# Attention output matrix of branch B built in natural row order and put into q's order by transfers within SBUF

## The chip, the cores and the metric

The kernel runs on one core of one Trainium2 chip. The metric is device time in microseconds: the median of the runs, and for reading, one profiled execution with every instruction of every engine. TensorE (PE) multiplies matrices and writes to PSUM only; PEld is its weight load, which overlaps the matmuls. VectorE (DVE) and ScalarE (ACT) compute on SBUF and PSUM, GpSimd (POOL) works only at the start, and SyncE (SP) issues most of the DMA transfers. Every engine works through its own queue in order.

## The reference

Two linear-attention blocks, A and B, share the input x (2048 tokens, 640 features) and are mixed by a gate. Each has 32 heads of 20 features.

```python
def _A_ref(x, wqkv, wo):              # _B_ref is the same with B's weights
    qkv = (x @ wqkv).reshape(B, S, 3, H, Dh).transpose(2, 0, 3, 1, 4)
    q, k, v = qkv[0], qkv[1], qkv[2]
    phi = lambda t: jnp.where(t > 0, t + 1, jnp.exp(t)) + 1e-6
    pq, pk = phi(q), phi(k)
    kv = jnp.einsum("bhsd,bhse->bhde", pk, v)
    z = jnp.einsum("bhsd->bhd", pk)
    num = jnp.einsum("bhqd,bhde->bhqe", pq, kv)
    den = jnp.einsum("bhqd,bhd->bhq", pq, z)[..., None] + 1e-6
    return (num / den).transpose(0, 2, 1, 3).reshape(B, S, D) @ wo

x = A_x
g = sigmoid((x * gate_w).sum(-1, keepdims=True))
return g * _A_ref(x, A_wqkv, A_wo) + (1 - g) * _B_ref(x, B_wqkv, B_wo)
```

## The kernel before

The kernel never forms v. For each branch it computes G = x^T phi(k) (640 by 640, tiles `GT`), then per head kv = wv^T G, then M = blockdiag(kv) @ wo (640 by 640, tiles `M[0]` and `M[1]`). The gate and the reciprocal of the denominator are multiplied into phi(q), which lies transposed in `pqT[0]` and `pqT[1]` (features on partitions, five chunks). The result is then pqA @ M_A + pqB @ M_B, a product with inner size 1280.

**q's order.** Chunk c, partition p of `pqT` holds feature 5p + c (`mixed`, L246). M must have its rows in the same order: natural row r belongs on partition r // 5, chunk r % 5.

**M_A** (`kv_a` L430, `m_a` L448) is made among the key chunks of branch B. Heads are taken in blocks of six, six and four to each half of the features (`WB`, 120, 120 and 80 rows): 30 matmuls give the kv blocks in PSUM, four VectorE multiplications with the mask put them into `KVA`, and for each of the six blocks two matmuls of 320 columns give rows of M_A in natural order. ScalarE copies a block to a stage in `GT`, SP writes it to a scratch tensor in DRAM (L461), and a last transfer (L463) loads all of it in q's order.

**M_B** is made later, between the last Strassen product of G (`g_strassen`, L330) and the products of the last stage. Groups of four heads are used (`KG` = 80): `kvt_mm` (L413) makes four blocks per half, 20 matmuls, `kvt_mask` (L422) masks them into `KVT`, and `m_half` (L472) makes 128 rows of one chunk in q's order directly, with eight matmuls 32 columns wide per half (80 in all), whose weights take every fifth column. ScalarE (one half: VectorE) copies them to `M[1]`.

**The last stage** computes the product of inner size 1280 by Winograd's form of Strassen's scheme. Tokens are split into lower and upper 1024, the inner size into A and B, the columns into two halves of 320. A `Pair` (L573) holds tokens i*128 of the lower and of the upper half; there are eight pairs, with seven products of five matmuls each (`prod`, L559):

- P1 = pqA(lower) by M_A's left half; P2 = pqB(lower) by M_B's left half; P3 = s4 by M_B's right half; P4 = pqB(upper) by TM3; P5 = s1 by TM0; P6 = s2 by TM1; P7 = D3 by TM2.
- s1, s2, s4 are sums of parts of `pqT`, which `p_sums` (L509) makes for two pairs at a time as its k = 1, 2, 4 (VectorE, 128x1280); s2 and s4 lie in `xT`. TM0 to TM3 are sums of M's quarters (`m_sums`, L520; TM0 at L740).
- P1's result is copied by ScalarE to `p1s` and P6 accumulates onto it in the same bank x; ScalarE copies that to `u2`; VectorE adds P7 to make `u3`, and four more sums (`c22`, `c11`, those of P4 and P3) make the four output quarters. P4 accumulates onto P7 in bank y, P3 onto P5 in bank z; P2 is in bank w.

There are eight PSUM banks: z, x, w and y, one for even and one for odd pairs. In this kernel each of the eight is a tile of its own (`acc`, L733 and L765). Before the w and y banks are opened, the pools `mid` and `single` use their space for kv and M_B; `kv` there is one tile of two banks. The tail from L700 on is under a manual schedule: each engine's queue has the order in which the lines are written.

## Time and profile before

| | |
|---|---|
| median of 3 runs | 189.83 us (189.77 to 190.37) |
| span of the profiled execution, first to last instruction | 188.1 us |
| PE busy | 182.7 us, 97% of the span, 1460 matmuls |
| PE weight loads | 123.5 us, 66% |
| DVE busy | 150.3 us, 80%, 244 instructions |
| ACT busy | 75.0 us, 40% |
| granted TensorE clock | 1.000 over the span |
| DMA | 15.63 MB, mean 83 GB/s |

The span is counted inside the device time; 1.7 us of the median lie around it. Busy time of PE is counted from modelled ends, so 97% means that its queue is nearly always supplied. The chain of waits follows the work that ended last back to its start; in the timeline a line gives start, duration, engine, source line, operation, tiles written and read, shape, and in brackets the idle time before it and what ended that.

### The profile page before, as it was taken

What the parts mean: (1) busy time and instruction counts of PE and PEld (TensorE: products, weight loads), DVE (VectorE), ACT (ScalarE), POOL (GpSimd) and SP (SyncE); (2) the same over time, 40 slices, a digit from 0 to 9 for tenths busy, and PEclk for the clock granted to TensorE, in tenths of its full rate; (3) what the DMA queues carried; (4) which work ended last, traced back from release to release, by engine and by line L of the source; (5) the groups of instructions that cost most, each with busy time, mean ns of one, the idle gap of its engine ahead of it and who ended that gap; (6) DMA issues with size and microseconds to landing.
All of it is one profiled execution on the core that took longest, in us unless ns stands there. A gap on an engine that the chain in (4) does not pass through costs nothing.

```text
span 188.1 us, 3574 instructions
## 1 busy us (share of the span) xinstructions
PE 182.7 (97%) x1460; PEld 123.5 (66%) x1465; DVE 150.3 (80%) x244; ACT 75.0 (40%) x106; POOL 2.8 (2%) x17
## 2 busy tenths in 40 slices
PE   8899999999999999999999999999999999999992
PEld 3566657755577677877765555576778776777772
DVE  1378968899998999799889997739699989787553
ACT  2055446457942501367674577422401611111110
POOL 6000000000000000000000000000000000000000
PEclk9999999999999999999999999999999999999999
DMA  5975447992140000011115000000543003211222
GB/s 184 320 124 94 105 84 250 360 249 87 16 164 0 3 0 0 3 33 33 54 44 189 2 0 0 3 0 0 178 112 62 3 3 112 97 70 56 87 71 71
DMA packets 19802, 15.63 MB, mean 83 GB/s; under 512 B 9546, under 2 KB 19658, under 8 KB 19786
## 3 DMA queue, kind: packets, MB, share of 16 engines
q1 hardware_dynamic: 18922, 14.59, 29.0%
q10 hardware_dynamic: 864, 0.82, 1.3%
q8 instruction: 11, 0.18, 0.4%
q14 instruction: 5, 0.04, 0.1%
HBM read 10.00 MB, written 3.44 MB: 71 GB/s over the span
## 4 chain that ended last, share of the span: by engine, by line
PE 93%; DMA 3%; DVE 1%; ACTq 0%; issue 0%; ACT 0%; DVEq 0%
PE gs L325 16%; PE kB L207 12%; PE qB L256 11%; PE kA L207 11%; PE qA L256 7%; PE ox L563 6%; PE oy L563 5%; PE oz L563 5%; PE qA L267 5%; DMA xn<-in_A_x_dram 3%; PE ow L563 3%; PE gB L298 2%; PE gA L298 2%; DVE osb L568 1%; PE mA L456 1%; PE mid L417 1%
## 5 line engine op out<-in xcount | busy, mean ns | idle before, releaser
L207 PEld LDWEIGHTS <-xT 128*128 128x128 bf16 x320 | 31.0, 98 | 12.4 <-DVE xT L192 0.5
L200 DVE TENSOR_SCALAR e<-e 128x640 bf16<-128x640 bf16 (+1 forms) x52 | 18.7, 360 | 6.3 <-ACT e L197 5.7
L207 PE MATMUL kB<-wkB,xT 128*128 128x320 bf16 x160 | 23.0, 299 | 0.0
L207 PE MATMUL kA<-wkA,xT 128*128 128x320 bf16 x160 | 22.6, 299 | 0.1
L256 PE MATMUL qB<-xT,wqB 128*128 128x512 bf16 x98 | 21.7, 379 | 0.1
L197 ACT ACTIVATE e<-kB 128x640 bf16<-128x640 f32 x16 | 11.3, 704 | 18.8 <-PE kB L207 17.5
L256 PEld LDWEIGHTS <-wqB 128*128 128x128 bf16 x100 | 11.7, 117 | 9.8 <-issue 0.2
L197 ACT ACTIVATE e<-kA 128x640 bf16<-128x640 f32 x16 | 11.0, 704 | 13.3 <-PE kA L207 13.3
L204 DVE SCALAR_TENSOR_TENSOR pk<-kA,e 128x640 bf16<-128x640 f32 x16 | 13.2, 825 | 1.7
L204 DVE SCALAR_TENSOR_TENSOR pk<-kB,e 128x640 bf16<-128x640 f32 x16 | 13.2, 825 | 1.7
L197 ACT ACTIVATE e<-qA 128x1024 bf16<-128x1024 f32 x10 | 10.2, 1023 | 9.3 <-PE qA L267 3.7
L197 ACT ACTIVATE e<-qB 128x1024 bf16<-128x1024 f32 x10 | 10.2, 1023 | 8.7 <-PE qB L256 8.4
L256 PE MATMUL qA<-xT,wqA 128*128 128x512 bf16 x59 | 13.2, 379 | 0.1
L607 ACT COPY u<-ox 128x320 f32<-128x320 f32 x8 | 3.4, 425 | 21.9 <-PE ox L563 21.9
L325 PEld LDWEIGHTS <-S 128*128 128x128 bf16 x96 | 9.4, 98 | 3.6
L325 PEld LDWEIGHTS <-xn 128*128 128x128 bf16 x96 | 9.1, 98 | 4.0 <-issue 0.4
L256 PEld LDWEIGHTS <-wqA 128*128 128x128 bf16 x60 | 7.0, 117 | 5.8
L563 PEld LDWEIGHTS <-xT 128*128 128x128 bf16 x85 | 8.0, 98 | 3.1 <-DVE xT L502 0.2
L591 ACT COPY p1s<-ox 128x320 f32<-128x320 f32 x8 | 3.4, 426 | 16.6 <-PE ox L563 16.6
L563 PEld LDWEIGHTS <-pqTA 128*128 128x128 bf16 x85 | 7.9, 98 | 2.9 <-issue 0.2
L563 PEld LDWEIGHTS <-pqTB 128*128 128x128 bf16 x80 | 7.8, 98 | 3.0
L325 PE MATMUL gs<-pk,xn 128*128 128x320 bf16 x64 | 9.4, 300 | 0.0
(124 smaller groups left out, 285.2 us busy)
## 6 DMA issues: line engine op xcount, KB each, us to landing
out_dram<-osb SPq DMA_DIRECT2D x14, 160.0 KB, 1.8
xn<-in_A_x_dram SPq DMA_DIRECT2D x3, 640.0 KB, 6.8
wqA<-in_A_wqkv_dram SPq DMA_DIRECT2D x1, 800.0 KB, 7.3
wvA<-in_A_wqkv_dram SPq DMA_DIRECT2D x1, 800.0 KB, 11.8
wkB<-in_B_wqkv_dram SPq DMA_DIRECT2D x1, 800.0 KB, 6.3
wqB<-in_B_wqkv_dram SPq DMA_DIRECT2D x1, 800.0 KB, 4.8
MA<-ma_dram SPq DMA_DIRECT2D x1, 800.0 KB, 4.3
wvB<-in_B_wqkv_dram SPq DMA_DIRECT2D x1, 800.0 KB, 5.7
```

The lines of the kernel that those rows point to most:

```text
L197: nc.scalar.activation(out=e[:], in_=src, func=ACT.Exp)
L200: nc.vector.tensor_scalar(e[:], e[:], 1.0, EPS, op0=ALU.min, op1=ALU.add)
L204: nc.vector.scalar_tensor_tensor(out=dst, in0=src, scalar=1.0 + EPS, in1=e[:], op0=ALU.add, op1=ALU.max)
L207: nc.tensor.matmul(pt[:, hf, 0:HF], lhsT=xT[:, c, i * P:(i + 1) * P], rhs=wk[b][:, c, hf * HF:(hf + 1) * HF], start=(c == 0), stop=(c == D ...
L256: nc.tensor.matmul(pt[:, u, :], lhsT=mixed(wq[b][:, c, :], m), rhs=xT[:, c, n * HB:(n + 1) * HB], start=(c == 0), stop=(c == DT - 1),)
L267: nc.tensor.matmul(pt[:, u, :], lhsT=mixed(wq[b][:, c, :], m + u), rhs=xT[:, c, n * HB:(n + 1) * HB], start=(c == 0), stop=(c == DT - 1),)
L298: nc.tensor.matmul(pt[:, hf, 0:HF], lhsT=xn[:, i, c * P:(c + 1) * P], rhs=pk[:, i, hf * HF:(hf + 1) * HF], start=(i == 0), stop=(i == ST - 1),
L325: nc.tensor.matmul(pt[:, n, 0:HF], lhsT=left[:, i, n * P:(n + 1) * P], rhs=right[:, i, :], start=(first and i == 0), stop=(i == hc - 1), s ...
L417: nc.tensor.matmul(pt[:KG, hf, j * KG:(j + 1) * KG], lhsT=wv[b][:, c, (4 * hf + j) * KG:(4 * hf + j + 1) * KG], rhs=GT[hf][:, c, j * KG:(j ...
L563: nc.tensor.matmul(dst, lhsT=left[:, c, r0:r0 + P], rhs=right[:, c, :], start=(first and c == 0), stop=(c == DT - 1), skip_group_check=not ...
L591: nc.scalar.copy(out=self.p1s[:], in_=self.at("x"))
L607: nc.scalar.copy(out=self.u2[:], in_=self.at("x"))
```

## The change

- M_B is made as M_A is: `kv_mm` and `kv_mask` (blocks of 120, 120, 80 rows, into `KVA`), then `m_rows` for each of six blocks: two matmuls, a copy of the rows to a stage (in `pk`, free by then), and one transfer from SBUF to SBUF that puts 120 or 80 rows on 24 or 16 partitions of `M[1]`, in q's order. The copies are ACT's, DVE's, ACT's, DVE's, ACT's, and for the last block one half each.
- M_A uses the same function: its rows go from SBUF to `M[0]` directly, without the scratch tensor in DRAM and the load from it.
- The eight PSUM banks of the last stage are opened at once, as four tiles z, x, w, y of two banks each; `acc` holds their halves. kv of B and the six blocks use them first.
- P1 of pairs 2, 3 and 4 is moved ahead of the first P2, into free halves of w and y. Its result is kept in `pk`, and P6 of these pairs no longer accumulates onto it: VectorE adds P6 and `p1s` to make `u2`, in place of ScalarE's copy.
- TM0 is made earlier, in `g_all` ahead of `rec_pass`; the other TM sums are three instructions over the whole tile where there were fifteen by chunks.
- wo of B is loaded by four transfers in place of one; `KVT`, its memset and the scratch tensor go.

```diff
@@
-KG = 80
-NG = 8
...
-    KVT = persist.tile([P, 4, 3, KG], BF16, name="KVT")
...
-    ma_dram = scratch.tile([D, D], BF16, name="ma_dram")
...
-    nc.vector.memset(KVT[:], 0.0)
...
@@ -410,75 +404,54 @@
         )
         return zsel
 
-    def kvt_mm(b, pt, hf):
-
-        for j in range(4):
+    def kv_mm(b, hf, dst):
+
+        for i, w in enumerate(WB):
+            d0 = i * WB[0]
             for c in range(DT):
                 nc.tensor.matmul(
-                    pt[:KG, hf, j * KG:(j + 1) * KG], lhsT=wv[b][:, c, (4 * hf + j) * KG:(4 * hf + j + 1) * KG],
-                    rhs=GT[hf][:, c, j * KG:(j + 1) * KG], start=(c == 0), stop=(c == DT - 1),
+                    dst[:w, d0:d0 + w], lhsT=wv[b][:, c, hf * HF + d0:hf * HF + d0 + w],
+                    rhs=GT[hf][:, c, d0:d0 + w], start=(c == 0), stop=(c == DT - 1),
                 )
 
-    def kvt_mask(pt, hf):
-
-        nc.vector.tensor_tensor(
-            out=KVT[:KG, 2 * hf:2 * hf + 2, 0:3:2, :],
-            in0=pt[:KG, hf, 0:HF].rearrange("p (g k n) -> p g k n", g=2, k=2),
-            in1=maskE[:KG, None, None, 0:KG].to_broadcast([KG, 2, 2, KG]), op=ALU.mult,
-        )
+    def kv_mask(hf, src):
+
+        for i, n in ((0, 2), (2, 1)):
+            w = WB[i]
+            nc.vector.tensor_tensor(
+                out=KVA[:w, 3 * hf + i:3 * hf + i + n, 0:w],
+                in0=src[:w, i * WB[0]:i * WB[0] + n * w].rearrange("p (i n) -> p i n", i=n),
+                in1=maskE[:w, None, 0:w].to_broadcast([w, n, w]), op=ALU.mult,
+            )
 
     def kv_a():
 
         pt = ps("kvA")
         for hf in range(2):
-            for i, w in enumerate(WB):
-                d0 = i * WB[0]
-                for c in range(DT):
-                    nc.tensor.matmul(
-                        pt[:w, hf, d0:d0 + w], lhsT=wv[0][:, c, hf * HF + d0:hf * HF + d0 + w],
-                        rhs=GT[hf][:, c, d0:d0 + w], start=(c == 0), stop=(c == DT - 1),
-                    )
+            kv_mm(0, hf, pt[:, hf, :])
         for hf in range(2):
-            for i, n in ((0, 2), (2, 1)):
-                w = WB[i]
-                nc.vector.tensor_tensor(
-                    out=KVA[:w, 3 * hf + i:3 * hf + i + n, 0:w],
-                    in0=pt[:w, hf, i * WB[0]:i * WB[0] + n * w].rearrange("p (i n) -> p i n", i=n),
-                    in1=maskE[:w, None, 0:w].to_broadcast([w, n, w]), op=ALU.mult,
-                )
-
-    def m_a(k):
+            kv_mask(hf, pt[:, hf, :])
+
+    def m_rows(b, k, pt, stage, engines):
 
         hf, i = divmod(k, 3)
-        w, d0 = WB[i], hf * HF + i * WB[0]
-        pt = ps("mA")
+        w, p0 = WB[i], (hf * HF + i * WB[0]) // DT
         for n in range(2):
             nc.tensor.matmul(
-                pt[:w, n, 0:HF], lhsT=KVA[:w, k, 0:w], rhs=wo_sb[0][:w, k, n * HF:(n + 1) * HF], start=True, stop=True,
+                pt[:w, n, 0:HF], lhsT=KVA[:w, k, 0:w], rhs=wo_sb[b][:w, k, n * HF:(n + 1) * HF], start=True, stop=True,
             )
-        part = GT[k % 2][:, k // 2 % 2 * 2:k // 2 % 2 * 2 + 2, :]
-        nc.scalar.copy(out=part[:w], in_=pt[:w, :, 0:HF])
-        nc.sync.dma_start(out=ma_dram[d0:d0 + w, :], in_=part[:w].rearrange("p b n -> p (b n)"))
-        if k == NW - 1:
-            nc.sync.dma_start(out=M[0][:], in_=ma_dram[:].rearrange("(p c) f -> p c f", c=DT))
-
-    def m_unit(b, c, eng, pt=None):
-
-        pt = ps("mA") if pt is None else pt
-        for hf in range(2):
-            m_half(b, c, hf, pt[:, hf, 0:HF])
-        evac(M[b][:, c, :], pt, eng)
-
-    def m_half(b, c, hf, dst):
-
-        for k in range(2):
-            for g in range(4):
-                heads = KVT[:KG, g, k:k + 2, :].rearrange("p x n -> p (x n)")
-                nc.tensor.matmul(
-                    dst[32 * g:32 * g + 32, :], lhsT=mixed(heads, c),
-                    rhs=wo_sb[b][:KG, 2 * g + k, hf * HF:(hf + 1) * HF], start=(k == 0), stop=(k == 1),
-                    tile_position=(0, 32 * g),
-                )
+        if len(engines) == 1:
+            copy = nc.scalar.copy if engines[0] == "act" else nc.vector.tensor_copy
+            copy(out=stage[:w], in_=pt[:w, :, 0:HF])
+        else:
+            for n, eng in enumerate(engines):
+                copy = nc.scalar.copy if eng == "act" else nc.vector.tensor_copy
+                copy(out=stage[:w, n], in_=pt[:w, n, 0:HF])
+        nc.sync.dma_start(out=M[b][p0:p0 + w // DT, :, :], in_=stage[:w].rearrange("p b n -> p (b n)"))
+
+    def m_a(k):
+
+        m_rows(0, k, ps("mA"), GT[k % 2][:, k // 2 % 2 * 2:k // 2 % 2 * 2 + 2, :], ("act",))
 
     def rec_pass(b, zsel, slot):
 
@@ -517,18 +490,14 @@
             if k in ks:
                 add_rows(dst, a, b, op)
 
-    def m_sums(cs, ks=(2, 1, 3)):
+    def m_sums():
 
         lo, hi = slice(0, HF), slice(HF, D)
-        for k in ks:
-            for c in cs:
-                a, b = M[0][:, c, :], M[1][:, c, :]
-                if k == 1:
-                    add_rows(TM[1][:, c, :], b[:, hi], TM[0][:, c, :], ALU.subtract)
-                elif k == 2:
-                    add_rows(TM[2][:, c, :], b[:, hi], a[:, hi], ALU.subtract)
-                else:
-                    add_rows(TM[3][:, c, :], b[:, lo], TM[1][:, c, :], ALU.subtract)
+        a, b = M[0], M[1]
+        for dst, left, right in (
+            (TM[2], b[:, :, hi], a[:, :, hi]), (TM[1], b[:, :, hi], TM[0][:]), (TM[3][:], b[:, :, lo], TM[1])
+        ):
+            add_rows(dst, left, right, ALU.subtract)
 
     def norm_spread(b, rts, slots):
 
@@ -585,10 +554,15 @@
         def at(self, bank):
             return acc[bank][self.i % 2][:, 0:HF]
 
-        def p1(self):
-            prod(self.at("x"), pqT[0][:, :, 0:SH], M[0][:, :, 0:HF], self.i, True)
-            self.p1s = work.tile([P, HF], FP32, tag="e", name="p1s", bufs=3)
-            nc.scalar.copy(out=self.p1s[:], in_=self.at("x"))
+        def p1(self, early=None):
+            dst = self.at("x") if early is None else early[:, 0:HF]
+            prod(dst, pqT[0][:, :, 0:SH], M[0][:, :, 0:HF], self.i, True)
+            self.early = early is not None
+            if self.early:
+                self.p1s = pk[:, NW + self.i, :].bitcast(FP32)
+            else:
+                self.p1s = work.tile([P, HF], FP32, tag="e", name="p1s", bufs=3)
+            nc.scalar.copy(out=self.p1s[:], in_=dst)
 
         def p2(self):
             prod(self.at("w"), pqT[1][:, :, 0:SH], M[1][:, :, 0:HF], self.i, True)
@@ -602,9 +576,12 @@
             prod(self.at("y"), D3, TM[2], self.i, True)
 
         def p6(self):
-            prod(self.at("x"), xT[:, :, 0:SH], TM[1], self.i, False)
+            prod(self.at("x"), xT[:, :, 0:SH], TM[1], self.i, self.early)
             self.u2 = tmp("u2", "ex")
-            nc.scalar.copy(out=self.u2[:], in_=self.at("x"))
+            if self.early:
+                out_add(self.u2[:], self.at("x"), self.p1s[:])
+            else:
+                nc.scalar.copy(out=self.u2[:], in_=self.at("x"))
             self.u3 = tmp("u3", "zr")
             out_add(self.u3[:], self.at("y"), self.u2[:])
 
@@ -643,18 +620,14 @@
         return t
 
     def load_wo(b, eng):
-        if b == 0:
-            t = wo_sb[0] = wpool.tile([P, NW, D], BF16, tag="wo", name="woA")
-            for hf in range(2):
-                for i, n in ((0, 2), (2, 1)):
-                    w, d0 = WB[i], hf * HF + i * WB[0]
-                    eng.dma_start(
-                        out=t[:w, 3 * hf + i:3 * hf + i + n, :],
-                        in_=wo_dram[0][d0:d0 + n * w, :].rearrange("(j p) f -> p j f", p=w),
-                    )
-            return
-        wo_sb[b] = wpool.tile([P, NG, D], BF16, tag="wo", name="woB")
-        eng.dma_start(out=wo_sb[b][:KG], in_=wo_dram[b].rearrange("(j p) f -> p j f", p=KG))
+        t = wo_sb[b] = wpool.tile([P, NW, D], BF16, tag="wo", name=f"wo{'AB'[b]}")
+        for hf in range(2):
+            for i, n in ((0, 2), (2, 1)):
+                w, d0 = WB[i], hf * HF + i * WB[0]
+                eng.dma_start(
+                    out=t[:w, 3 * hf + i:3 * hf + i + n, :],
+                    in_=wo_dram[b][d0:d0 + n * w, :].rearrange("(j p) f -> p j f", p=w),
+                )
 
     def q_pass(b, units, sums, lifted):
 
@@ -666,6 +639,8 @@
     def g_all(b):
 
         zsel = g_pass(b, DT - 1, 1)
+        if b == 1:
+            add_rows(TM[0][:], M[0][:, :, HF:D], M[0][:, :, 0:HF], ALU.subtract)
         rts = rec_pass(b, zsel, 2)
         g_strassen(b, lambda: norm_spread(b, rts, (2, 3)))
 
@@ -730,43 +705,36 @@
         TM[1], TM[2] = t[:, 0], t[:, 1]
         part = [slice(n * RB, (n + 1) * RB) for n in range(4)]
         half = ST // 2
-        acc = {k: [bank(outer, f"o{k}{n}") for n in range(2)] for k in "zx"}
+        two = {k: bank(outer, f"o{k}", 2) for k in "zxwy"}
+        acc = {k: [t[:, n] for n in range(2)] for k, t in two.items()}
         pairs = [Pair(i) for i in range(half)]
-        with late_pool("mid") as mid:
-            first = bank(mid, "mid0", 2)
-            kv = bank(mid, "mid1", 2)
-            kvt_mm(1, kv, 0)
-            kvt_mask(kv, 0)
-            add_rows(TM[0][:], M[0][:, :, HF:D], M[0][:, :, 0:HF], ALU.subtract)
-            pairs[0].p1()
-            kvt_mm(1, kv, 1)
-            kvt_mask(kv, 1)
-            p_sums(part[0], (1, 2))
-            pairs[1].p1()
-            m_unit(1, 0, "act", first)
-            m_unit(1, 1, "act", bank(mid, "mid1", 2))
-            m_sums((0, 1), (2, 1))
-        with late_pool("single") as single:
-            for hf in range(2):
-                m_half(1, 2, hf, acc["z"][hf][:, 0:HF])
-                nc.scalar.copy(out=M[1][:, 2, hf * HF:(hf + 1) * HF], in_=acc["z"][hf][:, 0:HF])
-            m_sums((2,), (2, 1))
-            m_unit(1, 3, "act", bank(single, "s3", 2))
-            m_sums((3,), (2, 1))
-            pts = [bank(single, f"s4{hf}")[:, 0:HF] for hf in range(2)]
-            for hf in range(2):
-                m_half(1, 4, hf, pts[hf])
-            nc.scalar.copy(out=M[1][:, 4, 0:HF], in_=pts[0])
-            nc.vector.tensor_copy(out=M[1][:, 4, HF:D], in_=pts[1])
-            m_sums((4,), (2, 1))
+
+        def m_b(k, bank2, *engines):
+            m_rows(1, k, two[bank2], pk[:, k, :].rearrange("p (b n) -> p b n", b=2), engines)
+
+        kv_mm(1, 0, acc["y"][0])
+        kv_mask(0, acc["y"][0])
+        pairs[0].p1()
+        p_sums(part[0], (1,))
+        kv_mm(1, 1, acc["y"][1])
+        kv_mask(1, acc["y"][1])
+        m_b(0, "w", "act")
+        m_b(1, "z", "dve")
+        pairs[1].p1()
+        m_b(2, "y", "act")
+        m_b(3, "w", "dve")
+        m_b(4, "z", "act")
+        m_b(5, "y", "act", "dve")
+        p_sums(part[0], (2,))
+        pairs[2].p1(acc["w"][0])
         for p in pairs[0:2]:
             p.p5()
-        inner = ctx.enter_context(late_pool("inner"))
-        acc |= {k: [bank(inner, f"o{k}{n}") for n in range(2)] for k in "wy"}
+        pairs[3].p1(acc["w"][1])
+        pairs[4].p1(acc["y"][0])
+        p_sums(part[0], (4,))
+        m_sums()
         for p in pairs[0:2]:
             p.p2()
-        p_sums(part[0], (4,))
-        m_sums(range(DT), (3,))
         for p in pairs[0:2]:
             p.p7()
             p.p6()
@@ -782,7 +750,7 @@
                 p.p6()
                 p.p5()
                 p.c22()
-            if after is not None:
+            if i > 3 and after is not None:
                 after.p1()
             if i == 1:
                 p_sums(part[1], (1,))
```

More of the change, by code (lines that the diff above doesn't have):

```diff
@@ L53 @@
     work = ctx.enter_context(tc.tile_pool(name="work", bufs=2))
-    scratch = ctx.enter_context(tc.tile_pool(name="scratch", bufs=1, space=bass.MemoryType.DRAM))
     banks = ctx.enter_context(ExitStack())
```

## The prediction

> **What bounds the kernel now.** I read the engine totals, then the chain of waits in order of time, then the timeline of the stretch that the change touches, its windows, and the DMA issues.
>
> The chain is one unbroken run of TensorE work from 7 us to 182 us. Its pieces around the change (start, length, what):
>
> ```profile
> 142.06 0.76 PE mid L417 x20
> 142.82 0.68 PE ox L563 x5
> 143.50 0.86 PE mid L417 x20
> 144.36 0.68 PE ox L563 x5
> 145.04 1.22 PE mid L477 x32
> 146.26 0.54 PE oz L477 x16
> 146.81 1.09 PE s L477 x31
> 147.89 1.47 PE oz L563 x10
> 149.36 1.36 PE ow L563 x10
> ```
>
> The reader should see three things. A product of the last stage costs 0.68 us. The three L477 pieces, M_B, cost 2.85 us. And the two halves of L417 are the same 20 matmuls, yet the second takes 0.10 us longer. The timeline shows why:
>
> ```profile
> 142.91 0.48 DVE L424 TENSOR_TENSOR KVT<-mid,maskE 80x320 bf16<-80x320 f32 x1
> 143.21 1.03 PEld L417 LDWEIGHTS <-wvB 128*80 128x80 bf16 x20
> 143.44 0.92 PE L417 MATMUL mid<-GT,wvB 128*80 128x80 bf16 x20
> ```
>
> The weights of the second half are in at 143.33 and its GT has been complete since 142.99 (the last L378 sum, 142.10 + 0.89), but its first matmul starts at 143.44, just after the mask of the first half has ended (143.39). Mask and matmul share one thing: the tile `kv`, of two PSUM banks, of which the mask reads bank 0 and the matmul writes bank 1. So here **a write to one bank waits for a read of the other bank of the same tile**. The semaphore events agree: where ACT copies GT bank by bank (L294, 125.07), TensorE signals once, after the second bank's last matmul, and not 0.14 us earlier for the first. Where banks are tiles of their own (the halves of L752 and L759), there are two signals.
>
> After this stretch VectorE is nearly full too:
>
> ```profile
> 149.20:158.00 8.80, 8.80 (x67) 6.26 (x64) 7.94 (x21) 1.28 (x3) 0.00 (x0) 1.00 0.11 39
> 158.00:170.00 12.00, 12.00 (x90) 8.63 (x89) 10.14 (x20) 2.31 (x6) 0.00 (x0) 1.00 0.24 82
> ```
>
> (PE, PEld, DVE, ACT, POOL busy, clock, DMA share, GB/s.) TensorE is busy throughout at clock 1.00, so a gap there is lost time. How one product is followed:
>
> ```profile
> 152.11 0.42 ACT L607 COPY u<-ox 128x320 f32<-128x320 f32 x1 [3.47 <-PE ox L563]
> 152.57 0.49 DVE L568 TENSOR_TENSOR u<-oy,u 128x320 f32<-128x320 f32 x1 [0.76 <-ACT u L607]
> 153.10 0.49 DVE L568 TENSOR_TENSOR osb<-oz,u 128x320 bf16<-128x320 f32 x1
> 157.19 0.81 DVE L502 TENSOR_TENSOR xT<-pqTA 128x1280 bf16<-128x1280 bf16 x1
> 158.06 0.85 PE L563 MATMUL ox<-TM,xT 128*128 128x320 bf16 x5
> ```
>
> P6(0) starts at 151.23, its copy u2 0.88 later, the sum u3 from 152.57 to 153.06: P6's start plus 1.83. And P6(2) at 158.06 starts 0.06 after its s2 sum ends: VectorE has no slack there even now.
>
> **TensorE's own work, 141.90 to the first P2.** Before: 7.29 us (141.90 to 149.19, timeline), with two P1 and two P5. After, in order: first kv half 0.75 (L437's 30 matmuls took 1.49); P1(0) 0.68; a wait of 0.18, because the mask is now two instructions (at L444 0.54 from start to end: 142.91 to 143.45); second half 0.75; M_B blocks 0 and 1, 0.54 (two matmuls, 0.27, as L456 in the chain); P1(1) 0.68; blocks 2 to 4, 0.82; then block 5. It writes tile y, whose block 2 ACT must have copied: ACT has p1s(1) until 146.11, then a copy of 0.69 (as L460) to 146.80, while TensorE is ready at 146.30. Wait 0.56, block 0.27. Then P1(2), P5(0), P5(1), P1(3), P1(4): 3.40. Sum 8.63, P2(0) at 150.53. That holds three P1 more (2.04), so 7.29 + 2.04 - 8.63 = **0.70 us gained** (2.85 - 1.63 from M_B, less waits).
>
> **The rows.** An SBUF to SBUF transfer is not in the trace. Nearest rows:
>
> ```profile
> ma_dram<-GT SPq DMA_DIRECT2D x4, 150.0 KB, 2.0
> ma_dram<-GT SPq DMA_DIRECT2D x2, 100.0 KB, 1.7
> MA<-ma_dram SPq DMA_DIRECT2D x1, 800.0 KB, 4.3
> woB<-in_B_wo_dram SPq DMA_DIRECT2D x1, 800.0 KB, 5.7
> ```
>
> I take 2.0 (same rows, same size; 80 rows 1.8), bounds 1.7 and 4.3. SP issues one in 0.31 to 0.36 and nothing else is queued there until the stores at 155.8. The last copies end at 147.82, the rows are in by 149.67, so P2(0) has 0.86 us of cover (P1 and P5 products). A shorter transfer gains nothing; 4.3 costs 1.44. Sums TM2, TM1, TM3 as whole-tile instructions (TM0's row: 0.98 each) run 149.73 to 152.75; P7(0) needs the first at 151.9, P6(0) the second at 152.6, P4(0) the third after 154: hidden, cover 1.2, 0.9 and over 1 us.
>
> **Edits at nothing, and their cover.** TM0 (0.98) goes ahead of L492, where VectorE idles 1.72 us (124.57 to 126.29). M_A's rows land directly, one load of 4.3 us fewer, needed 20 us later. wo of B comes in four loads: the same 800 KB at 137.75, alone on the queue, so 5.7 plus three issues, about 144.5 for the last part; block 0's comes first and is used at 144.3, block 5's at 146.9. The other near row is woA's 11.2, excluded because those loads stood behind 2.7 MB issued just before them, while here wvB has landed by 136.4. The memset of KVT (0.46 at 1.0 us) had no waiter. VectorE's new copies of blocks 1 and 3 (640 wide, taken as 0.82 by the 640-wide PSUM sum at L342; 0.48 by the 320-wide copy L760) end before their banks are wanted.
>
> **The two-bank tiles.** Now z, x, w and y are tiles of two banks, halves used by even and odd pairs; before, each half was its own tile. By the kv row, a product into one half waits until the other's last read is done. In order from P2(0) 150.53, P7(0) 151.89, P6(0) 152.57:
> - P7(1) writes y, which u3(0) reads until P6(0) + 1.83 = 154.40; plus 0.06 it starts at 154.46 instead of 153.25: **1.21**.
> - P4(0) writes y, read by u3(1) until P6(1) 155.14 + 1.83; starts 157.03 instead of 155.82: **1.21**.
> - P7(2) writes y, read by P4(1)'s sum. VectorE from 157.05: c22, c11, two sums of pair 0, then k=1 0.73, c11 0.40, k=2 0.73, and that sum at 160.85 to 161.33. TensorE is ready at 160.43: **0.96**.
> - The early pairs 2 to 4 make u2 on VectorE (0.49 for ACT's 0.43, then u3). P4(3) waits for u3(3): **0.48**; P1(5) for u2(4) in tile x: **0.50**.
> - P7(3) to P7(7): each 1.36 after the last P4, whose sum ends 0.88 + 0.48 + 0.06 = 1.42 after it: 0.06 each, **0.31**.
> - At the end P3(7) is cut into z's two banks; the second now waits for the first's sum (0.51 matmul, 0.04, 0.31, 0.06, less 0.35 already spent): **0.62**.
>
> Together 5.29, less 0.04 that P6(2) waits today. Sum: 5.29 - 0.04 - 0.70 = **4.55 us longer**. The profiled span of 188.1 becomes 192.7; the median of the runs lies 1.7 above the span, so 189.83 + 4.55 = **194.4 us**.
>
> The Trainium skill (Perfetto Trace Analysis, Matmuls) says that independent matmul groups should rotate through PSUM banks, so that the evacuation of one overlaps the next group's matmuls; by it the pairs would go on overlapping, bank by bank, and the time would be that of the first rival. The kv row differs, for banks of one tile.
>
> **Rivals.**
> 1. *Banks of a tile are told apart* (against it the kv wait and the single signals; for it that all of these are in short stretches). Then VectorE's queue decides: u3(0) at 153.91 starts the same unbroken run as today's 152.57 to 158.00 (5.43), so s2 is ready at 159.34 while P6(2), without a P1 ahead of it, is wanted at 158.65: 0.70 to 0.75; u2 on VectorE makes P4(2) wait 0.43 and P4(3) 0.54. 1.72 - 0.04 - 0.70 = +0.98: **190.8 us**.
> 2. *Faster: TensorE alone sets the end.* Banks are told apart, and VectorE keeps up, because its pieces turn out some 0.7 us shorter before P6(2) and 0.5 in each of pairs 2 and 3; from less than that on it decides. Left is the 0.70 gained: **189.1 us**. Against it: VectorE 7.94 of 8.80 busy, while the change adds three sums and takes three P1 out of its cover.
> 3. *Rows late*: the transfer takes 4.3, as the load of MA; on top of the forecast 1.44: **195.8 us**. Against it: that row moved five times the bytes.
> 4. The change doing nothing is excluded: L477 goes.
>
> **How the numbers follow.** Forecast 0.77, rival 1 0.10, rival 2 0.06, rival 3 0.07. The forecast's own range is 193.2 to 195.8 (P7(2), P4(3) and P1(5) hang on VectorE's exact order, about 1 us). To reach 8 in 10 with a margin I go down to rival 1 and up past rival 3: 190.2 to 196.2. 0.3% is about what a measurement here tells from no change (0.57 us). Faster: rival 2, 0.06; within: the near part of rival 1, 0.03; slower the rest, 0.91.
>
> **What would show it.** Gaps of about 1.2 us on TensorE ahead of the second P7 and the first P4, each ended by a VectorE sum on `oy`; small ones before each later P7; a gap between the halves of the last P3. L456 should read 24 matmuls and the M_B rows land about 2 us from issue. Wrong it would be if P7(1) follows P6(0) without a gap: then rival 1 is read at P6(2), and rival 2 if that has none either. A gap at P2(0) ended by a DMA is rival 3.

## The result, and the profile after

The changed kernel takes **198.97 us** (median, 198.20 to 200.14), the kernel before beside it 189.96 (189.61 to 190.56): a ratio of 1.0476, 95% interval 1.0446 to 1.0505. It is slower, as forecast, by 9.0 us and not by 4.55, and above the range of 190.2 to 196.2. Line numbers below are those of the changed kernel: L412 is `kv_mm`, L421 its mask, L440 the matmuls of `m_rows`, L445 and L449 its copies, L450 its transfer, L475 `add_rows`, L532 `prod`, L537 `out_add`, L584 the copy u2. Kernels of the experiments can differ from them by a few.

The page of the changed kernel: the span, the engine totals, the granted clock in 40 slices, and the transfers of rows (number, KB of each, median us from issue to landing):

```profile
span 196.9 us, 3436 instructions
PE 185.1 (94%) x1387; PEld 123.2 (63%) x1387; DVE 152.4 (77%) x238; ACT 73.0 (37%) x101; POOL 2.8 (1%) x17
PEclk9999999999999999999999999999999699999999
MA<-GT SPq DMA_DIRECT2D x2, 100.0 KB, 2.7
MB<-pk SPq DMA_DIRECT2D x2, 100.0 KB, 4.1
```

TensorE has fewer matmuls and is busy for longer: one slice, about 153 to 157 us, has a clock of 0.6. And the same kind of transfer lands after 2.7 us for M_A, after 4.1 for M_B.

Three things make up the time. **The shared tiles** come first in size. The timeline, each line with the idle time before it and what ended that:

```profile
158.89 0.84 PE L532 MATMUL oy<-TM,D 128*128 128x320 bf16 x5 [1.04 <-DVE u L537]
161.50 0.84 PE L532 MATMUL oy<-TM,pqTB 128*128 128x320 bf16 x5 [1.09 <-DVE u L537]
165.87 0.84 PE L532 MATMUL oy<-TM,D 128*128 128x320 bf16 x5 [0.81 <-DVE osb L537]
173.21 0.84 PE L532 MATMUL oy<-TM,pqTB 128*128 128x320 bf16 x5 [0.32 <-DVE u L537]
```

These are P7(1), P4(0), P7(2) and P4(3). The bracket counts from a modelled end of the matmul before. Measured from the start of one matmul to the start of the next, where 0.14 us is the normal step, the four lose 1.20, 1.26, 0.97 and 0.48 us; P1(5) loses 0.51, the second half of the last P3 0.68 (its half-width matmuls have a step of 0.07), and six smaller ones of 0.05 to 0.07 together 0.38. In all 5.48 us.

**The rows** come second. The timeline around them:

```profile
145.16 4.86 SPq L450 DMA_DIRECT2D MB<-pk  x6
147.38 0.49 DVE L449 CAST pk<-oy 80x320 bf16<-80x320 f32 x1 [0.54 <-ACT pk L449]
153.30 2.32 PE L532 MATMUL ow<-MB,pqTB 128*128 128x320 bf16 x10 [2.85 <-DMA MB<-pk]
```

The last copy ends at 147.87, but SP is still issuing until 150.02, because a transfer of 120 rows keeps it for 0.77 to 0.81 us and one of 80 rows for 0.61. Block 5's is issued at 149.41, and the chain of waits gives what follows:

```profile
149.41 3.54 DMA MB<-pk
152.95 0.35 issue
153.30 2.32 PE ow L532 x10
155.62 1.33 PE oy L532 x5
156.95 0.91 PE ox L532 x5
```

The rows are in at 152.95, P2(0) starts at 153.30, and TensorE, whose last early P1 began at 149.61, could have started at 150.29: a stop of 3.01 us, 0.35 of it after the landing.

**The clock** comes third. In the same lines ten P2 matmuls take 2.32 us where 1.36 to 1.53 is the rule, and five of P7 take 1.33 instead of 0.68. The windows (stretch, us, PE, PEld, DVE, ACT, POOL busy, clock, DMA share, GB/s) say why:

```profile
150.60:153.30 2.70, 0.00 (x0) 0.03 (x1) 0.07 (x1) 0.31 (x1) 0.00 (x0) 1.00 0.26 56
153.30:153.90 0.60, 0.60 (x5) 0.44 (x6) 0.60 (x1) 0.00 (x0) 0.00 (x0) 0.96 0.00 0
153.90:157.10 3.20, 3.20 (x14) 1.76 (x13) 2.22 (x3) 0.00 (x0) 0.00 (x0) 0.50 0.00 0
```

The clock is 1.00 during the stop and goes to 0.50 some 0.6 us after TensorE has begun again, for 3.4 us (153.85 to 157.27; the third window lies within). The 20 matmuls of the two P2, P7 and P6 take 4.39 us instead of 2.72: 1.67 us lost.

**The sum.** From the first kv matmul to the start of the last matmul the kernel before needs 42.61 us (141.90 to 184.51) and the changed one 52.05 (141.62 to 193.67): 9.44 more. The parts: tiles 5.48 - 0.04, M_B -0.65, stop 3.01, clock 1.67, together 9.47. The start, 0.28 earlier, and a tail 0.36 shorter make 8.8 between the spans. This stretch is used for every run below, since the loads at the beginning move the start of it by up to 1.3 us between executions.

### The profile page after: what moved, and what is told of

Its sections match the earlier page's. It is cut to its first block, busy times and chain, and to the rows that moved or that the text cites. A ratio compares the mean times of both kernels' runs of the same rounds, so it can differ in the third digit from the quotient of the medians.

```text
span 196.9 us, 3436 instructions
## 1 busy us (share of the span) xinstructions
PE 185.1 (94%) x1387; PEld 123.2 (63%) x1387; DVE 152.4 (77%) x238; ACT 73.0 (37%) x101; POOL 2.8 (1%) x17
## 4 chain that ended last, share of the span: by engine, by line
PE 84%; DVE 7%; DMA 4%; ACT 2%; issue 1%; SPq 0%; ACTq 0%; DVEq 0%
PE gs L319 16%; PE kB L201 11%; PE qB L250 11%; PE kA L201 11%; PE qA L250 7%; PE oy L532 5%; PE qA L261 4%; PE ox L532 4%; PE oz L532 3%; DMA wkA<-in_A_wqkv_dram 3%; PE gA L292 2%; PE gB L292 2%; PE ow L532 2%; DVE osb L537 2%; DVE xT L475 2%; DMA MB<-pk 2%
## 5 line engine op out<-in xcount | busy, mean ns | idle before, releaser
L532 PEld LDWEIGHTS <-pqTB 128*128 128x128 bf16 x80 | 7.9, 100 | 8.1 <-issue 5.0
L565 ACT COPY p1s<-ox 128x320 f32<-128x320 f32 x5 | 2.1, 426 | 28.6 <-PE ox L532 28.6
L532 PEld LDWEIGHTS <-xT 128*128 128x128 bf16 x85 | 8.3, 99 | 3.9 <-issue 0.7
L532 PEld LDWEIGHTS <-pqTA 128*128 128x128 bf16 x85 | 8.0, 98 | 3.5 <-issue 0.8
L537 DVE TENSOR_TENSOR osb<-oz,u 128x320 bf16<-128x320 f32 (+1 forms) x18 | 8.2, 453 | 2.5 <-PE oz L532 1.7
L532 PE MATMUL ow<-MB,pqTB 128*128 128x320 bf16 x40 | 7.4, 324 | 2.9 <-DMA MB<-pk 2.9
```

What stands on the lines that cost most here:

```text
L532: nc.tensor.matmul(dst, lhsT=left[:, c, r0:r0 + P], rhs=right[:, c, :], start=(first and c == 0), stop=(c == DT - 1), skip_group_check=not ...
L537: nc.vector.tensor_tensor(out=dst, in0=acc, in1=sb, op=ALU.add)
L565: nc.scalar.copy(out=self.p1s[:], in_=dst)
```

## The experiments

Time is the median with its lowest and highest, the stretch is that of the profiled execution (before: 42.61), the stop is the one ahead of P2(0), and the clock the mean of the profiled execution.

| run | us | ratio (95%) | stretch | stop | clock |
|---|---|---|---|---|---|
| changed kernel | 198.97 (198.20 to 200.14) | 1.0476 (1.0446 to 1.0505) | 52.05 | 3.01 | 0.991 |
| e1_own_banks | 195.22 (193.77 to 196.26) | 1.0232 (1.0158 to 1.0307) | 48.63 | 3.34 | 0.989 |
| e2_filled_gap | 197.15 (196.52 to 197.87) | 1.0360 (1.0313 to 1.0407) | 50.39 | filled | 1.000 |
| e3_two_queues | 200.25 (199.19 to 201.49) | 1.0524 (1.0465 to 1.0584) | 53.65 | 3.67 | 0.978 |
| e4_row_probe | 189.31, one run | none | | | 1.000 |
| e5_more_cover | 193.53 (192.77 to 194.24) | 1.0198 (1.0166 to 1.0230) | 46.35 | 1.17 | 1.000 |
| e6_rows_by_dram | 201.74 (200.54 to 202.26) | 1.0622 (1.0584 to 1.0661) | 55.73 | 5.89 | 0.983 |
| e7_early_p1_alone | 191.17 (190.49 to 191.47) | 1.0073 (1.0048 to 1.0098) | 44.25 | none | 0.998 |
| e8_repaired | 191.90 (191.48 to 192.31) | 1.0113 (1.0091 to 1.0134) | 45.39 | 1.33 | 1.000 |
| e9_one_transfer | 194.17 (193.88 to 195.42) | 1.0236 (1.0196 to 1.0276) | 47.74 | 0.43 | 0.999 |
| e10_spread | 190.67 (190.09 to 191.79) | 1.0043 (1.0017 to 1.0068) | 43.75 | none | 1.000 |
| e11_half_rows | 195.59, one run | none | 49.05 | 1.70 | 0.997 |
| e12_order | 190.25 (189.59 to 190.66) | 1.0011 (0.9996 to 1.0027) | 43.36 | none | 1.000 |

### The tiles: e1_own_banks

```diff
-        two = {k: bank(outer, f"o{k}", 2) for k in "zxwy"}
-        acc = {k: [t[:, n] for n in range(2)] for k, t in two.items()}
+        acc = {"x": [bank(outer, f"ox{n}") for n in range(2)]}
+        mid = ExitStack()
+        mid_pool = mid.enter_context(late_pool("mid"))
+        two = {k: bank(mid_pool, f"m{k}", 2) for k in "zwy"}
+        acc["y"] = [two["y"][:, n] for n in range(2)]
...
         m_b(5, "y", "act", "dve")
+        mid.close()
+        inner = ctx.enter_context(late_pool("inner"))
+        acc |= {k: [bank(inner, f"o{k}{n}") for n in range(2)] for k in "zwy"}
```

> The changed kernel, but after M_B's copies the six banks of z, w and y are opened again as six tiles of one bank (x too). Theory (a product into one half of a two-bank tile waits for the last read of the other half): the gaps ahead of P7(1), P4(0), P7(2), P4(3), P1(5), of each later P7 and inside the last P3 go, 5.4 us in the changed kernel's trace; VectorE's queue gives back 0.7 at P6(2), 0.4 at P4(2) and 0.5 at P4(3), so some 3.7 us shorter than the changed kernel, about 195.3 us. The wait at P2(0), 2.85 us, stays. Rival (VectorE is simply full and the tiles don't matter): P7(1) still starts 1.2 us late, and the time changes by less than 1 us.

The ratio falls from 1.0476 to 1.0232, and in the last stage none of the gaps of the shared tiles is left. The timeline of e1 has P7(2) without a gap, and three gaps that VectorE's queue makes, 0.77, 0.41 and 0.55 us between starts, before P6(2), P4(2) and P4(3): the gaps of the first rival.

```profile
163.88 0.84 PE L532 MATMUL oy<-TM,D 128*128 128x320 bf16 x5
165.32 0.85 PE L532 MATMUL ox<-TM,xT 128*128 128x320 bf16 x5 [0.61 <-DVE xT L475]
...
167.78 0.84 PE L532 MATMUL oy<-TM,pqTB 128*128 128x320 bf16 x5 [0.24 <-DVE u L537]
...
172.40 0.84 PE L532 MATMUL oy<-TM,pqTB 128*128 128x320 bf16 x5 [0.38 <-DVE u L537]
```

So the same program with one tile to a bank has the rival's waits, and with two banks to a tile the forecast ones: the tile is what is waited for. The stretch is 52.05 - 48.63 = 3.42 us shorter: 5.48 gone, 1.73 come, and 0.33 more of stop make 3.42.

### The clock: e2_filled_gap

```diff
         pairs[4].p1(acc["y"][0])
+        for _ in range(4):
+            prod(acc["w"][1][:, 0:HF], pqT[0][:, :, 0:SH], M[0][:, :, 0:HF], 3, True)
         p_sums(part[0], (4,))
```

> The changed kernel with the P1 product of pair 3 repeated four times (2.7 us of TensorE work, result not used) into the same bank while TensorE waits for M_B's rows. Theory (the granted clock falls to 0.5 from 153.9 to 157.1 because TensorE stood idle for 3 us): the clock stays at 1.00, the 20 matmuls after the wait take 2.7 instead of 4.4 us, the time falls by 1.6 us to about 197.3; the rows still land at about 153. Rival (the clock falls for another reason, or the wait and the slow clock are independent): clock 0.5 again and no change.

TensorE is given work that nobody needs while it waits for the rows. The clock stays at 1.000 and the chain after the wait reads as it did before the change:

```profile
153.12 1.52 PE ow L532 x10
154.64 0.68 PE oy L532 x5
155.32 0.69 PE ox L532 x5
```

Against the changed kernel's 2.32, 1.33 and 0.91 for the same products. The time falls by 198.97 - 197.15 = 1.8 us, the stretch by 1.66. The lower clock is thus what follows a TensorE that stands still, not something that the P2 matmuls bring with them.

How long it must stand still shows across the runs. Stops of 1.17, 1.33 and 1.70 left the clock at 1.00; with 3.01 and 3.34 came 3.4 us of 0.50, with 3.67 and 5.89 6.8 us. The Trainium skill (TensorE: Matmul & The Clock Gate, HAM oscillation — how this bites in real kernels) gives the rule as no idle gaps of TensorE over about 3.4 us. Here 3.01 us was enough, so the measurement decides for a lower figure. Nor does it come every time: of e1's four executions two had a mean clock of 1.000 and took 193.8 and 194.2 us, two had 0.989 and 0.991 and took 196.3 and 196.2. (The profiled one of these also began the stretch 1.1 us later.) One execution of the changed kernel had 1.000 too and still took 198.2; what it lost in place of the clock was not seen.

The traces show more of the rule than the length of a stop. In each of the 13 that hold the clock, it changes only at whole steps of 3.41 us: the first stretch at 1.00 is 43, 44, 54, 55 or 56 steps long, and the half clock inside a kernel one step or two. The windows of e3, one step each:

```profile
149.34:152.75 3.41, 1.23 (x10) 0.67 (x7) 0.25 (x1) 0.85 (x2) 0.00 (x0) 1.00 0.75 103
152.75:156.16 3.41, 2.08 (x8) 1.20 (x9) 2.06 (x3) 0.00 (x0) 0.00 (x0) 0.50 0.00 0
156.16:159.57 3.41, 3.41 (x13) 1.82 (x12) 0.82 (x1) 0.00 (x0) 0.00 (x0) 0.50 0.00 0
159.57:162.98 3.41, 1.52 (x11) 0.97 (x10) 1.68 (x4) 0.85 (x2) 0.00 (x0) 1.00 0.00 0
```

After a step with 1.23 us of TensorE work the clock falls, here 1.3 us before P2(0) starts at 154.08; after one with 1.52 us it stays at 1.00. In the other traces too it fell after steps at full clock with at most 1.40 us of work (0.56 in the changed kernel, 1.35 in e1), and not after those with 1.52 or more. So what counts is the idle time within one step, some 2 us of 3.41, and a stop of 3.3 us that a step's end cuts in two can go unpunished. That this is what kept the clock in two of e1's executions is not shown: there is no trace of them.

### The rows: e9_one_transfer, e11_half_rows, e4_row_probe

Three runs ask what of the rows' lateness is the single transfer and what is six of them. In e9 only block 5 is transferred, with the other five blocks made as before (the other rows hold what its space held for the product G, not zeros):

```diff
-        nc.sync.dma_start(out=M[b][p0:p0 + w // DT, :, :], in_=stage[:w].rearrange("p b n -> p (b n)"))
+        if b == 0 or k == NW - 1:
+            nc.sync.dma_start(out=M[b][p0:p0 + w // DT, :, :], in_=stage[:w].rearrange("p b n -> p (b n)"))
```

> The changed kernel with only the last of M_B's six row transfers left (560 of the 640 rows of M_B stay zero). Theory (the one term of the forecast that was mis-sized is the rows; with it comes the slow clock): alone, the last transfer lands some 2.7 us after its issue at 147.9, by 150.6, P2(0) waits at most 0.4 us, the clock stays at 1.00, the gaps before P7 and P4 stay as they are: 194.4 us, the time that was forecast. Rival (a single transfer within SBUF is as late, 3.5 us or more from issue): a stop of over 1 us and 195.5 or more.

```profile
147.91 0.62 SPq L452 DMA_DIRECT2D MB<-pk  x1
150.69 1.53 PE L534 MATMUL ow<-MB,pqTB 128*128 128x320 bf16 x10 [0.26 <-DMA MB<-pk]
```

In this timeline of e9 the issue follows the copy at once, the rows are in at 150.64, and P2(0) loses 0.43 us. All gaps of the shared tiles are as in the changed kernel (1.20, 1.26, 0.97, 0.48, 0.51). Time 194.17 and span 192.5: with five of the six row transfers out of the way, the kernel runs at what was forecast for it (194.4 and 192.7). In the stretch it is 5.13 longer than the kernel before: the forecast's 4.55, the stop of 0.43 and 0.15 of small terms.

e11 keeps six transfers and halves their bytes:

```diff
+        if b == 1:
+            nc.sync.dma_start(out=M[1][p0:p0 + w // DT, :, 0:HF], in_=stage[:w, 0])
+            return
```

> The changed kernel with all six transfers, each of the left 320 columns only: as many rows, half the bytes (the right half of M_B stays zero). Theory (what a transfer within SBUF costs goes by its rows: 0.6 us of issue for 80, 0.8 for 120, whatever their length): issues and landing as in the changed kernel, the last rows in at about 153. Rival (the bytes set the pace, 12 engines at a time): the rows in by 151.5.

All of the view of the tile M_B (issue time in ns, least, median, most; then landing), the changed kernel first:

```profile
L450 SPq DMA_DIRECT2D MB<-pk x6: 609/775/806, 145.2 to 149.4; - x6
DMA to landing us min/median/max: 4.1/4.1/4.1
```

```profile
L452 SPq DMA_DIRECT2D MB<-pk x6: 610/776/805, 145.2 to 149.5; - x6
DMA to landing us min/median/max: 3.7/3.7/3.7
```

Issue is the same to a nanosecond, so here it goes by rows (0.61 for 80, 0.78 for 120), not by bytes. The last rows land 2.18 us after their issue instead of 3.54, at 151.65, near the rival's 151.5, so that part does go by bytes, or by how much the earlier transfers have left undone.

e4 measures one transfer by itself: to the kernel before it adds two of 120 rows in a quiet stretch, with the data not used.

```diff
+            if b == 1 and k == 0:
+                nc.sync.dma_start(out=pqT[1][0:24, :, SH:SH + D], in_=pqT[1][:120, 0, 0:D])
+            if b == 1 and k == 2:
+                nc.sync.dma_start(out=pqT[1][0:120, 4, SH:SH + D], in_=pqT[1][:120, 2, 0:D])
```

> The kernel before with two added transfers from SBUF to SBUF in a quiet stretch of the DMA queues (branch B's q chunks, some 98 to 108 us): 120 rows of 1280 bytes, first onto 24 partitions (five rows each, the form of the change), then onto 120 partitions (the form of the write to DRAM). Theory A (going onto 24 partitions is what is slow): the first is issued in 0.78 us and lands after 3.3, the second in 0.31 and lands after 2.0. Theory B (any transfer within SBUF is slow): both like the first. Time of the kernel unchanged.

SP's timeline in e4, first 80 rows of M_A to DRAM:

```profile
97.59 0.31 SPq L461 DMA_DIRECT2D ma_dram<-GT  x1
...
103.00 0.95 SPq L664 DMA_DIRECT2D pqTB<-pqTB  x1
107.72 0.86 SPq L666 DMA_DIRECT2D pqTB<-pqTB  x1
```

The transfer onto 24 partitions is in at 106.12, 3.1 us after issue; the one onto 120 partitions, no reordering, at 110.40, 2.7 us after. So putting 5 rows on a partition is not what is slow. A transfer of 120 rows from SBUF to SBUF takes SP 0.86 to 0.95 us and lands after 2.7 with nothing beside it, after 3.1 where the load of M_A was still landing until 103.64; 120 rows of M_A to DRAM took 0.32 to 0.36 and landed after 2.0 (median). M_A's direct rows in the changed kernel, 3 us apart, give the same issue: 0.77 to 0.96 for 120 rows.

### Other ways to bring the rows: e3_two_queues, e6_rows_by_dram

```diff
-        nc.sync.dma_start(out=M[b][p0:p0 + w // DT, :, :], in_=stage[:w].rearrange("p b n -> p (b n)"))
+        eng = nc.gpsimd if b == 1 and k % 2 else nc.sync
+        eng.dma_start(out=M[b][p0:p0 + w // DT, :, :], in_=stage[:w].rearrange("p b n -> p (b n)"))
```

> The changed kernel with the row transfers of M_B blocks 1, 3 and 5 issued on GpSimd's queue, the others on SP's. Theory (six issues of 0.6 to 0.8 us one behind another on SP put the last at 149.4, 1.5 us after its copy): the last is issued at about 148, the rows are in at about 151.3 instead of 153.0, TensorE waits 1.2 instead of 2.9 us, and the time falls by 1.7 us, or 3.3 if the clock then does not fall: 195.6 to 197.3. Rival (the transfers themselves are the limit, 12 engines for 90 rows of 1280 bytes at a time): rows as late as before, no change.

Blocks 1, 3 and 5 are issued by the idle GpSimd. e3's view of the tile M_B:

```profile
L451 POOL DMA_DIRECT2D MB<-pk x3: 540/631/770, 146.0 to 148.3; - x3
...
DMA to landing us min/median/max: 4.3/5.6/5.7
```

The last issue is 1.1 us earlier, at 148.30, and the rows are in 0.9 us later, at 153.88. The theory that the issuing queue alone was at fault fell: a later landing took up all that the issue gave. SP's block 4, issued at 147.27, was complete only at 153.44, so it is not GpSimd's transfers alone that were slow.

e6 takes the way of M_A in the kernel before, six writes to DRAM and one load:

```diff
+        nc.sync.dma_start(out=mb_dram[p0 * DT:p0 * DT + w, :], in_=rows)
+        if k == NW - 1:
+            nc.sync.dma_start(out=M[b][:], in_=mb_dram[:].rearrange("(p c) f -> p c f", c=DT))
```

> The changed kernel with only M_B's rows taken by the old route: six writes to a DRAM tensor and one load in q's order. Theory (issues of 0.31 us and landings of 2.0, then a load of 4.3, from rows that are there at 147.9): the rows are in at about 154.2, 1.2 us later than within SBUF, so about 200.2 us. Rival (the six transfers within SBUF are so slow that the detour is faster): rows in before 152, under 198 us.

```profile
L456 SPq DMA_DIRECT2D mb_dram<-pk x6: 313/346/2206, 145.2 to 148.0; - x6
```

Issues to DRAM are short again (0.31 to 0.38) except the sixth, which kept SP for 2.2 us. The last write landed at 151.67, the load at 156.19, and the stop grew to 5.89 us. Blocks 3 and 4 landed after 4.1 us here, writes of 120 rows after 2.0 (median) in the kernel before, where they were further apart: transfers close together can be late toward DRAM too. Direct transfers are the better of the two.

### The early P1: e7_early_p1_alone, e5_more_cover

e7 is the kernel before with only P1(2) to P1(4) moved ahead of P2(0), and u2 of these pairs on VectorE:

```diff
+        pairs[2].p1(acc["w"][0])
+        pairs[3].p1(acc["w"][1])
+        pairs[4].p1(acc["y"][0])
         for p in pairs[0:2]:
             p.p2()
...
-            if after is not None:
+            if i > 3 and after is not None:
                 after.p1()
```

> The kernel before with one part of the change alone: P1 of pairs 2, 3 and 4 ahead of the first P2, their u2 made by VectorE. Its banks are tiles of their own and M_B is as before. Theory (VectorE's queue sets the pace once three P1 are taken out of its cover): gaps of 0.7 at P6(2), 0.4 at P4(2), 0.5 at P4(3), about 191.7 us. Rival (the products are only moved): no gap, 190.0.

The timeline of e7:

```profile
159.76 0.85 PE L563 MATMUL ox<-TM,xT 128*128 128x320 bf16 x5 [0.55 <-DVE xT L502]
162.22 0.84 PE L563 MATMUL oy<-TM,pqTB 128*128 128x320 bf16 x5 [0.24 <-DVE u L568]
```

P6(2) waits for a VectorE sum, P4(2) for u3; between starts 0.72 and 0.41, and P4(3) 0.55. Together 1.68, against 1.64 in the stretch. So this part of the change costs 1.4 us by itself, and helps only where it covers a stop.

e5 is e1 with P1(5), P1(6) and P1(7) moved ahead as well:

```diff
         pairs[4].p1(acc["y"][0])
+        pairs[5].p1(acc["w"][0])
+        pairs[6].p1(acc["w"][1])
+        pairs[7].p1(acc["y"][1])
```

> Tiles of one bank as in e1_own_banks, and P1 of pairs 5, 6 and 7 moved ahead of the first P2 as well (2.04 us more TensorE work while the rows are under way). Theory (what is lost at P2(0) is the time by which the rows outlast the products put ahead of them, and the slow clock comes only after a long stop): the gap at P2(0) falls from 3.3 to about 1.3 us and the time by 2.0, to 193.2 us, if the clock still falls; by 4.0, to 191.2, if a stop of 1.3 us leaves the clock alone. Rival (the products are only moved, and the wait moves with them): about 195 as e1_own_banks.

The stop falls by about their 2.04 us, from 3.34 to 1.17, and the clock stays at 1.000. The price is u2 on VectorE in three more pairs: gaps of 0.42, 0.55 and 0.59 before P4(4), P4(5) and P4(6), 1.56 us.

### Toward a version that is not slower: e8_repaired, e10_spread, e12_order

e8 is e5 with the sums of part 1 made in VectorE's idle time ahead of P2(0), and blocks 4 and 5 issued by ACT.

```diff
+        for k in (4, 5):
+            w, p0 = WB[k - 3], (HF + (k - 3) * WB[0]) // DT
+            nc.scalar.dma_start(out=M[1][p0:p0 + w // DT, :, :], in_=pk[:w, k, :])
...
         p_sums(part[0], (4,))
+        p_sums(part[1])
         m_sums()
```

> e5_more_cover, with the three sums for pairs 2 and 3 made by VectorE while it waits for the rows (3.8 us idle in the changed kernel), and the transfers of M_B blocks 4 and 5 issued on ScalarE's queue after all row copies. Theory (the loss is made of shared tiles, rows outlasting their cover, the clock after the stop, and VectorE's queue; each is met): last issue at about 148.2, rows in at about 151.9, P2(0) wanted at 152.3, no stop over 0.3 us, clock 1.00; TensorE's own work is 0.7 us less than in the kernel before: 189.3 us, a ratio of 0.996. Rival (the transfers and not their issue are late): the rows at 153, a stop of 0.7 us, 190.0 or more.

The gaps of P6(2) and P4(2) went. The stop did not (1.33), though the last issue began at 148.47: each of ACT's issues took 1.3 to 1.4 us, and the rows were in at 153.38. The rival held: the transfers themselves are late.

e10 starts the transfers earlier, with blocks 0 and 1 ahead of the second half of kv, and spreads the sums.

```diff
         m_b(0, "w", "act")
         m_b(1, "z", "dve")
+        kv_mm(1, 1, acc["y"][1])
+        kv_mask(1, acc["y"][1])
+        m_b(2, "w", "act")
         pairs[1].p1()
...
         p_sums(part[1])
+        p_sums(part[2], (1, 2))
         m_sums()
```

> e8_repaired, with five instead of three later sums in VectorE's idle time and the other four one to an iteration, and M_B blocks 0 and 1 made ahead of the second kv half, so that their rows start 0.7 us earlier. Theory: no gap ahead of any P4 (2.1 us in e8_repaired), the stop at P2(0) 0.6 instead of 1.3 us: 2.8 us less, 189.1 us, a ratio of 0.996. Rival (the six transfers end when they end, however early the first starts; or VectorE's queue binds elsewhere): 189.8 or more.

The rows are in by 152.58 and P2(0) waits no more. What is left is order, in e10's timeline:

```profile
147.10 0.43 PE L440 MATMUL my<-woB,KVA 80*80 80x320 bf16 x2 [0.65 <-DVE pk L445]
155.10 0.84 PE L533 MATMUL oy<-TM,D 128*128 128x320 bf16 x5 [0.78 <-DVE TM L476]
```

Block 5 waits 0.81 us for the copies of its banks, and P7(0) 0.94 for TM2, which stands behind the sums on VectorE.

e12 moves these:

```diff
-        p_sums(part[0], (1,))
         m_b(4, "z", "act")
-        m_b(5, "y", "act", "dve")
+        m_b(5, "w", "act", "dve")
...
+        p_sums(part[0], (1,))
...
-        pairs[2].p1(acc["w"][0])
+        pairs[2].p1(acc["y"][0])
...
-        p_sums(part[2], (1, 2))
         m_sums()
+        p_sums(part[2], (1,))
```

> This kernel is e10_spread with three things moved. Block 5 goes into the w banks, which block 2 has left, instead of the y banks, and P1(2) into a y bank (e10 waited 0.81 us before block 5 for the copies of y); block 5's rows are issued by SP behind block 3's, so that ACT issues only block 4's; and of part 2's sums the first now stands behind the three sums of M_B and the second in pair 1's iteration, where VectorE idled 0.87 us (in e10 TM2 started at 154.06 with the rows in by 152.58, and P7(0) waited 0.94 and P6(0) 0.22 for it). Theory: each of these gaps goes and nothing takes its place, except that P2(0) can't start before the rows are in (about 152.3, against a TensorE that is ready at 152.0). 190.67 - 0.94 - 0.22 - 0.5 = 189.0 us, the first version that is faster than the kernel before, by 0.4%. Rival: VectorE, with about 0.8 us more to do between the third sum of M_B and the second pair, makes P4(0) and P7(1) wait for u3, and the rows land no earlier than 152.6: then some 0.7 us of it comes back, and the time is 189.7, that of the kernel before. The 0.59 us before P4(6) stays with both.

```profile
146.88 0.84 PE L533 MATMUL oy<-MA,pqTA 128*128 128x320 bf16 x5 [0.37 <-DVE pk L445]
148.60 1.53 PE L533 MATMUL oz<-TM,pqTA 128*128 128x320 bf16 x10 [0.88 <-DVE pqTA L476]
```

The gaps that it aimed at went, and two took their place, in e12's timeline above: P1(2) waits 0.53 us for block 3's copy on VectorE, and P5(0) waits 1.04 for s1, the sum that had been moved behind block 5. Its ratio is 1.0011, interval 0.9996 to 1.0027: no difference from the kernel before that could be told. No version that ran is faster. Whether one that keeps s1 in its old place is, was not tried.

## Why the prediction was right and where it was wrong

**Right: the direction, and the mechanism named as the likeliest.** *The two-bank tiles* were worth 5.29 us by the forecast and 5.48 in the trace, gap by gap: P7(1) 1.21 and 1.20, P4(0) 1.21 and 1.26, P7(2) 0.96 and 0.97, P4(3) 0.48 and 0.48, P1(5) 0.50 and 0.51, the last P3 0.62 and 0.68 (the terms written for it add up to 0.57). One row of the trace of before, the kv matmul that starts as the mask of the other half ends, had carried the rule, on a wait of 0.10 us. e1 shows that it is the tile: with a tile for each bank the gaps go, and the first rival's three come, 0.77, 0.41 and 0.55 where 0.70 to 0.75, 0.43 and 0.54 were worked out. The Trainium skill (Perfetto Trace Analysis, Matmuls) advises rotating through PSUM banks so that evacuation overlaps the next matmuls; the trace agrees in e1, and not with two banks in one tile, where P7(1) came 1.20 us late.

**Right: TensorE's own work.** The gain was 0.70 by the forecast, 0.65 in the trace (waits of 0.19, 0.44 and 0.16 for 0.18, 0.56 and none). The copies on VectorE took 0.82 and 0.49, as taken from the nearest rows.

**Right: the edits at nothing.** TM0 ran from 124.24 to 125.23 while VectorE had nothing else. The last 100 KB part of wo of B landed 4.4 us after issue, M_A's direct rows of 100 KB after 2.7, and nobody waited for either.

**Wrong: "The rows".** This step of the prediction is the term that was mis-sized. It took 2.0 us for the landing, and 0.31 to 0.36 for SP's issue, from the row that moves the same bytes from SBUF to DRAM. Measured for SBUF to SBUF, issue is 0.61 (80 rows) to 0.81 (120). With six of them it no longer hides behind the copies: block 5's issue came 1.54 us after its copy. Its landing took 3.54 us where 1.85 had been used. By that the rows were in at 152.95 instead of 149.67: 0.05 + 1.54 + 1.69 = 3.28 us late. The cover of 0.86 turned into a stop of 3.01: 3.28 - 0.86, 0.24 because TensorE was ready sooner, and 0.35 from the landing to the first matmul. The third rival had this mechanism with a chance of 0.07 and a price of 1.44, from a landing of 4.3; its bound was too low, since it left the issues in series out (147.82 + 4.3 = 152.12, which by the forecast's own 150.53 costs 1.59 and not 1.44). e4 and e9 show what one transfer costs (2.7 to 3.1 us), e11 that issue goes by rows and that half the bytes land sooner. Why SP needs longer for this kind of transfer the runs don't say.

**Wrong by omission: no step held the clock.** Every view of the kernel before had 1.00, and a stop of 1.44 us, the largest that was considered, would have left it there (1.70 did in e11). A stop of 3.01 did not: 1.67 us more. e2 shows that this is the stop's doing.

Put together: the forecast's +4.55, 0.19 more from the tiles, 0.05 from M_B, 3.01 and 1.67 make +9.47, against 9.44 in the stretch. Of the 4.6 us that the median lies above the forecast, nearly all is the rows and the clock after them; e9, with one transfer, came to 194.17.

## What to carry to other kernels

Price a transfer by a row with the same source and the same target: the same 120 rows to DRAM took 0.32 to 0.36 us to issue, within SBUF 0.77 to 0.96, and six in a row cost the issues in series as well as the landing. Before splitting PSUM into tiles, ask who reads one bank while another is written; two banks in one tile made TensorE wait 5.5 us here. A stop of TensorE has a second price once it is long: about 3 us of waiting cost another 1.7 of half clock, so cover that shortens it to below 1.9 us (a step of 3.41 with 1.52 of work kept the clock) is worth more than its length.

## What the runs showed of the hardware that was not expected

- A transfer of 120 rows of 1,280 bytes from SBUF to SBUF: issue 0.77 to 0.96 us on SP as a rule (1.2 once in e2 and in e5), 0.63 to 0.77 on GpSimd, 1.41 to 1.60 on ACT while SP issued too. Landing, of 80 or 120 rows: after 2.7 to 3.1 alone (e4, e9), up to 4.1 among six that SP issues, 4.3 to 5.7 for those that GpSimd issued, 3.4 and 4.9 for two of ACT's.
- Half the bytes in as many rows left the issue as it was (776 against 775 ns) and brought the last rows 1.3 us earlier.
- The half clock came and went on a grid of 3.41 us: after a step with at most 1.40 us of TensorE work, not after one with 1.52 or more. So it began 0.6 us (changed kernel) and 1.4 us (e1) after work had begun again, but 1.3 and 1.7 us before that in e3 and e6.
